# Moving two start loads ahead of the start barrier, with eight zero products for 14, in a decode attention kernel

## The chip, the cores and the metric

The kernel runs on one core of a Trainium2 chip. Its time is device microseconds (us) of that core, measured over a few executions. The profile's span is a little shorter than the time (652.0 us against 653.45 in the run that was profiled before the change), so spans are compared with spans and times with times.

## The reference

One decode step: a layer norm of x (4 rows of 448), attention with 16 query heads over 8 K/V heads and a cache of 8192 positions, and a small MLP mixer as a gate.

```python
xn = _layernorm(x)                       # x: (4, 1, 448)
q = (xn @ wq)                            # 16 heads of 256
scores = einsum("bhqd,bhkd->bhqk", q, k) * 256 ** -0.5     # k, v: (4, 8, 8192, 256) bf16
s = einsum("bhqk,bhkd->bhqd", softmax(scores), v) ... @ wo
g = _silu(mixer_mlp(xn, w1, w2, w3, w4)) # two norms, gelu; S = 1, so the shifted parts are zero
return x + s * g
```

K and V are 4 x 8 pairs of 4 MB. Everything that is read once adds up to 279 MB.

## The kernel before

SyncE issues nearly all loads on one queue: wq (3.7 MB), w3 and w4, the K of the first two heads, most of wo, then in turn a K and a V of 4 MB, each as soon as its buffer is free. There are two K and two V buffers. A "head" below is one of the 32 pairs of batch row and K/V head. ScalarE loads x (3.5 KB) itself.

The engines' programs start with a barrier that the compiler library puts in: every engine runs a drain (which raises a "gather" semaphore) and then waits for GpSimd's release (in the trace before, drains from 0.00 to 0.32 us, release at 0.61). A helper moves the first loads into that part:

```python
def begin_ahead(nc, loads):
    ...
    for load in reversed(loads):
        at = next(n for n, i in enumerate(first)
                  if i.engine == load.engine and isinstance(i, mybir.InstDrain))
        first.insert(at + 1, load)      # after the engine's arrival, before its wait
```

```python
def prog_sp(sp):
    ahead.append(sp.sem_inc(S["pause"], 1))       # two semaphore steps
    ahead.append(take(sp, "pause"))               # that only take time
    ahead.append(sp.dma_start(vflat[1][:, 0:DK * HDH], A_wq...).then_inc(S["dwq"], 16))
    ...                                           # w3, w4
    load_k(0); load_k(1); load_wo(NLATE, HQ, "dwo")
    for h in range(2, NH):
        load_k(h)                                 # waits v_k: head h-2 is transposed
        load_v(h - 2)                             # waits v_v: V buffer is free
    ...                                           # last V in four pieces, last wo in three
    sp.wait_ge(S["v_out"], 1)
    store(sp, 0)
    take(sp, "dout", 16 * NDG)

def prog_act(act):
    ahead.append(act.dma_start(x_sb[:, :], x2d).then_inc(S["dx"], 16))
```

On TensorE (PE) a prologue computes q and the MLP; then `NWARM` products of zeros follow, which only keep the array busy until the first K has landed. They are there for its clock: in the trace before they are 427 ns apart until 28.1 us and 217 after, and the clock records have full clock from 28.14:

```python
for i in range(NWARM):        # 14
    pe.matmul(psv[0:PVW, 0:QW], pT[:, 0, 0:PVW], wq_sb[:, 0, 0:QW], start=True, stop=True)
```

Each head then transposes K (L604 before, L612 after: the change shifts the lines by 8), multiplies, and multiplies with V. The last head's part (`finish`) has filler products of the same kind between its steps, `f_warm(n)`, 14 in all.

## Time and profile before

| what | value | read from |
|---|---|---|
| time, median of 3 | 653.85 us (653.24 to 654.89) | runs |
| span | 652.0 us | page |
| DMA | 279 MB, 428 GB/s mean | page |
| first packets of wq on the 16 engines | 1.26 to 2.12 us | list of DMA packets |
| third K load issued | 41.77 us | timeline |
| last piece of wo landed | 649.13 us | landings |

Here are the page's head and its rows for the whole DMA, which give in 40 equal slices the busy share in tenths and the rate:

```profile
span 652.0 us, 22813 instructions
PE 550.5 (84%) x9937; PEld 470.7 (72%) x9937; DVE 276.9 (42%) x622; ACT 255.8 (39%) x364; POOL 3.6 (1%) x17
DMA  9999999999999999999999999999999999999997
GB/s 374 440 420 433 430 434 434 430 438 426 440 426 440 426 440 426 440 428 436 432 435 430 434 434 426 440 426 440 426 440 428 438 428 438 430 436 430 434 429 301
```

DMA is full from the first slice to the last, while PE has a sixth of the span left. The waits of SyncE's queue (line, what it waited for, us in total, times, longest) say the same from the other side:

```profile
SPq L237 <- DVEq L515: 460.3, 30, 38.4
SPq L245 <- DVEq L483: 132.4, 31, 19.5
SPq L216 <- DVE out_b L544: 20.0, 1, 20.0
```

SyncE waits 460 us for K buffers, but that starves nobody: a load is issued 25 to 30 us before it lands, and landings are 9.7 us apart. The third line is the wait for the output.

The start, from the timeline (start, duration, engine, line, what, count, and in brackets the idle time before it and what ended it):

```profile
0.21 0.56 ACTq L312 DMA_DIRECT2D x_sb<-in_A_x_dram  x1
0.24 0.41 SPq L222 DMA_DIRECT2D vb<-in_A_wq_dram  x1
0.78 0.34 SPq L226 DMA_DIRECT2D vb<-in_B_w_dram  x1
2.01 0.38 DVE L385 CAST x_f<-x_sb 4x448 f32<-4x448 bf16 x1 [0.60 <-DMA x_sb<-in_A_x_dram]
...
23.94 5.26 PE L596 MATMUL psv<-vb,pT 128*32 128x512 bf16 x14
...
30.07 1.05 PE L604 MATMUL pst<-ident_b,kn 128*128 128x128 bf16 x16 [0.87 <-PEq L278]
...
41.77 0.33 SPq L237 DMA_DIRECT2D kn<-in_A_k_cache_dram  x1
```

The zero products fill 23.9 to 29.2, the first transposes start at 30.07 when K has landed, and the third K is issued at 41.77 when head 0 is transposed. And the end, the chain that ended last:

```profile
648.14 1.55 PE pst L703 x24
649.69 0.02 issue
649.72 0.40 DVE res L542
...
650.13 0.38 DVE out_b L544
```

PE's last products wait for the last piece of wo (649.13), so VectorE's closing instruction (`res`) starts 0.58 us after that landing.

### The profile page before, as it was taken

The page shows a single profiled execution, that of the slowest core. Times are in us where ns is not written, and L with a number is a line of the kernel's source. Part 1 is how long each engine was busy: PE and PEld are TensorE (multiplying, and loading weights), DVE is VectorE, ACT ScalarE, POOL GpSimd, SP SyncE. Part 2 cuts the span into 40 slices and gives each one's busy share as a digit, 9 for nine tenths or more (in the row PEclk, how much of TensorE's full clock was granted, in tenths as well). Part 3 has the DMA queues.
Part 4 walks back from the last instruction along what each step waited for, and adds up shares of the span by engine and source line. Part 5 has one row for each costly group of instructions (what it writes and reads, how often), then busy time and mean ns, then how long its engine had stood idle before and what let it go on. Part 6 is the DMA issues. An engine that isn't in the chain of part 4 may idle for free. (4 is left out here: it accounts for less than half of the span.)

```text
span 652.0 us, 22813 instructions
## 1 busy us (share of the span) xinstructions
PE 550.5 (84%) x9937; PEld 470.7 (72%) x9937; DVE 276.9 (42%) x622; ACT 255.8 (39%) x364; POOL 3.6 (1%) x17
## 2 busy tenths in 40 slices
PE   2799997988887987888897888898888798878897
PEld 1487876987676876667787766787677688757774
DVE  7344544343343443434443444444344344434442
ACT  4144543443343443323443333444234344423440
POOL 2000000000000000000000000000000000000000
PEclk9998999888799898889987888988779987978999
DMA  9999999999999999999999999999999999999997
GB/s 374 440 420 433 430 434 434 430 438 426 440 426 440 426 440 426 440 428 436 432 435 430 434 434 426 440 426 440 426 440 428 438 428 438 430 436 430 434 429 301
DMA packets 12353, 279.13 MB, mean 428 GB/s; under 512 B 1204, under 2 KB 3256, under 8 KB 3768
## 3 DMA queue, kind: packets, MB, share of 16 engines
q1 hardware_dynamic: 12328, 278.99, 99.5%
q8 instruction: 7, 0.11, 0.1%
q10 hardware_dynamic: 16, 0.01, 0.0%
q14 instruction: 2, 0.02, 0.0%
HBM read 278.99 MB, written 0.00 MB: 428 GB/s over the span
## 5 line engine op out<-in xcount | busy, mean ns | idle before, releaser
L604 PE MATMUL pst<-ident_b,kn 128*128 128x128 bf16 x4096 | 342.7, 237 | 81.4 <-PEq L278 79.3
L309 ACT ACTIVATE kT<-pst 128x1024 bf16<-128x1024 bf16 x224 | 229.3, 1024 | 357.5 <-ACTq L278 356.3
L604 PEld LDWEIGHTS pst<-ident_b,kn 128*128 128x128 bf16 x4096 | 271.7, 107 | 87.2 <-issue 86.6
L307 DVE COPY kT<-pst 128x1024 bf16<-128x1024 bf16 x288 | 197.5, 691 | 261.1 <-DVEq L278 261.1
L616 PE MATMUL psc<-qc,kT 128*128 128x2 bf16 x4096 | 178.2, 164 | 0.0
L616 PEld LDWEIGHTS psc<-qc,kT 128*128 128x128 bf16 x4096 | 157.1, 98 | 28.7 <-issue 28.5
L655 PE MATMUL psv<-vb,pT 128*4 128x512 bf16 x1056 | 85.6, 378 | 0.0
L634 PE MATMUL psm<-sel,po 128*128 128x2 f32 x272 | 36.8, 257 | 0.5 <-PEq L278 0.5
L634 PEld LDWEIGHTS psm<-sel,po 128*128 128x128 f32 x272 | 34.8, 196 | 0.9 <-issue 0.9
L655 PEld LDWEIGHTS psv<-vb,pT 128*4 128x4 bf16 x1056 | 21.8, 82 | 15.0 <-issue 0.4
L466 DVE TENSOR_REDUCE rmax<-psc 128x2 f32<-128x128 f32 x32 | 9.3, 292 | 48.1 <-DVEq L278 48.1
L484 DVE COPY po<-psv 128x512 f32<-128x512 f32 x34 | 23.5, 691 | 4.0 <-DVEq L278 3.3
L331 ACT ACTIVATE pT<-psc,negb 128x64 bf16<-128x64 f32 x66 | 20.6, 332 | 5.4 <-ACTq L278 5.4
L471 DVE TENSOR_REDUCE gmax<-psm 2x1 f32<-2x128 f32 x32 | 8.9, 279 | 32.3 <-DVEq L278 32.3
L628 PEld LDWEIGHTS psm<-diag,ones_f 2*128 2x128 f32 x66 | 13.5, 253 | 6.3 <-issue 5.0
L628 PE MATMUL psm<-diag,ones_f 2*128 2x2 f32 x66 | 16.2, 313 | 1.1 <-PEq L278 0.9
L331 ACT ACTIVATION_READ_ACCUMULATOR pT<-psc,negb 128x1 f32 x66 | 13.6, 206 | 0.0
L624 PEld LDWEIGHTS psm<-ident_f,rmax 128*2 128x2 f32 x32 | 2.6, 80 | 14.0 <-issue 14.0
L646 PE MATMUL psm<-rowsum,ones_f 128*128 128x2 f32 x64 | 11.6, 251 | 0.0
L552 PE MATMUL pst<-ident_b,xn_b 4*128 4x4 bf16 x14 | 0.6, 161 | 11.5 <-DVE xn_b L379 6.8
L646 PEld LDWEIGHTS psm<-rowsum,ones_f 128*128 128x128 f32 x64 | 9.5, 188 | 0.0
L474 DVE TENSOR_SCALAR diag<-ident_f,gmax 2x2 f32<-2x2 f32 x32 | 6.9, 217 | 4.8 <-DVEq L278 1.1
(101 smaller groups left out, 101.1 us busy)
## 6 DMA issues: line engine op xcount, KB each, us to landing
kn<-in_A_k_cache_dram SPq DMA_DIRECT2D x32, 4096.0 KB, 25.5
vb<-in_A_v_cache_dram SPq DMA_DIRECT2D x31, 4096.0 KB, 30.5
vb<-in_A_wq_dram SPq DMA_DIRECT2D x1, 3584.0 KB, 11.4
vb<-in_B_w_dram SPq DMA_DIRECT2D x2, 1568.0 KB, 16.3
wo_sb<-in_A_wo_dram SPq DMA_DIRECT2D x1, 2688.0 KB, 43.3
kn<-in_A_v_cache_dram SPq DMA_DIRECT2D x1, 2048.0 KB, 24.7
kn<-in_A_v_cache_dram SPq DMA_DIRECT2D x1, 1024.0 KB, 26.7
kn<-in_A_v_cache_dram SPq DMA_DIRECT2D x2, 512.0 KB, 27.9
```

Source lines behind the costliest of these rows:

```text
L307: engine.tensor_copy(dst, src).then_inc(S["v_ev"], 1)
L309: engine.activation(dst, src, ACT.Copy).then_inc(S["a_ev"], 1)
L331: ins = act.activation(pv_p[:, :, hh], sc[:, :, hh], ACT.Exp, bias=negb[:, s, hh:hh + 1], scale=SCALE, accum_out=rowsum[:, s, hh:hh + 1])
L466: v.tensor_reduce(rmax[:, :], psc[h % 2][:, 0:NCH * REP].rearrange("p (k h) -> p h k", h=REP), AX.X, ALU.max).then_inc(S["v_rmax"], 1)
L471: v.tensor_reduce(gmax[:, :], psm[0:REP, 0:P], AX.X, ALU.max).then_inc(S["v_s"], 1)
L484: v.tensor_copy(po[:, slot], psv[:, 0:CP * DH]).then_inc(S["v_po"], 1)
L604: ins = pe.transpose(dst[:, t * P:(t + 1) * P], kn[:, h % 2, GC * j + kl, half * P:(half + 1) * P], ident_b[:, :])
L616: ins = pe.matmul(psc[h % 2][:, kk * REP:(kk + 1) * REP], kT[:, j % RING, t * P:(t + 1) * P], qc[:, h % 2, half, :], start=(half == 0), st ...
L628: pe.matmul(psm[:, P:P + REP], ones_f[0:REP, :], diag[:, :], start=True, stop=True).then_inc(S["p_m2"], 1)
L634: ins = pe.matmul(dst(dh)[:, 0:width], po[:, slot, i * DH + dh:(i + 1) * DH:NHALF], sel[:, i, 0:width], start=(i == 0), stop=(i == CP - 1))
L646: pe.matmul(psm[:, P + REP:P + 2 * REP], ones_f[:, :], rowsum[:, h % 2, :], start=True, stop=True)
L655: ins = pe.matmul(psv[o:o + CP * REP, 0:CP * DH], pT[:, h % 2, kk * REP:(kk + CP) * REP], src[:, kk:kk + CP, :].rearrange("p c d -> p (c d)"),
```

## The change

Its intent is to start the stream of loads earlier. The wq load stands ahead of SyncE's drain and without the two pause steps; the x load heads ScalarE's program, ahead of its drain (in the diff it is the first of the two `loads`, and `later` puts ScalarE's former first two instructions behind it); there are eight zero products; the two pause steps stand in SyncE's closing part.

```diff
-    first = blocks[0].instructions
-    for load in reversed(loads):
-        at = next(n for n, i in enumerate(first)
-                  if i.engine == load.engine and isinstance(i, mybir.InstDrain))
-        first.insert(at + 1, load)
+    first = list(blocks[0].instructions)
+    for n, load in enumerate(loads):
+        own = [i for i in first if i.engine == load.engine]
+        drain = next(i for i in own if isinstance(i, mybir.InstDrain))
+        if n == 0:
+            later = own[0:2]
+            first = [i for i in first if i not in later]
+            at = first.index(drain)
+            first[at:at] = later
+            at = first.index(later[0])
+        else:
+            at = first.index(drain)
+        first.insert(at, load)
@@
-    NWARM = 14
+    NWARM = 8
@@ prog_sp
-            ahead.append(sp.sem_inc(S["pause"], 1))
-            ahead.append(take(sp, "pause"))
-            ahead.append(sp.dma_start(
+            ahead.insert(1, sp.dma_start(
@@
+            sp.sem_inc(S["pause"], 1)
+            take(sp, "pause")
             sp.wait_ge(S["v_out"], 1)
@@ prog_act
-            ahead.append(act.dma_start(x_sb[:, :], x2d).then_inc(S["dx"], 16))
+            ahead.insert(0, act.dma_start(x_sb[:, :], x2d).then_inc(S["dx"], 16))
```

## The prediction

> **What bounds it.** The DMA engines. The page's 40 slices show DMA at 9 tenths in all but the last, at 426 to 440 GB/s nearly throughout; 279.0 MB are read. In the list of DMA packets all 16 engines are active together for 638.8 of 652.0 us. PE is busy 84% but waits: SyncE's queue holds its K loads 460 us for buffers, yet each 4 MB load lands 25 to 30 us after issue and landings come 9.7 us apart, so the queue is two to three loads deep. The time is: the first wq packet's start (1.26 us into the span), about 646 us of packets, and the tail (last wo piece lands at 649.1, then DVE, the store and its receipt until 652.0).
>
> **What the change does.**
> 1. wq load. Before, SyncE runs its drain at 0.00 and two semaphore steps, and issues wq at 0.24 us (timeline of SyncE). After, the load is its first instruction: issue at about 0.00, first packet at about 1.0. The whole DMA stream moves 0.24 us earlier.
> 2. Barrier. SyncE now arrives after its 0.41 us of issue and ScalarE after 0.56 us of x issue (start about 0.13), so at about 0.7 in place of 0.32 (PE was last). Release moves from 0.61 to about 0.85, the w3 issue from 0.78 to about 1.0. wq's packets keep the engines busy until 10.7, so this is off the path. I take it that the drain does not wait for the data of a load in flight: no trace here shows a drain behind a load.
> 3. Eight zero products for 14. The timeline shows the 14 spaced 427 ns (half clock) until 28.1 us and 217 ns after. After: about 3.4 us of them, ending near 27.4 instead of 29.2; PE then waits for the first K, which landed at 29.94. [...] With eight it may not be granted in time. Estimate: head 0's 16 groups at 0.65 us would take up to 2.4 us longer. The third K load is issued when head 0's transposes are done, at 41.8; its packets start about 1.0 later, and the loads before it end at 44.35 (first engine) to 46.24 us (last). So 2.4 us of delay is absorbed where it counts: the last engine, which sets the time, doesn't idle.
> 4. The two semaphore steps move to where SyncE waits 20 us for the output: free.
>
> **On the path:** only the 0.24 us of step 1, and perhaps a few tenths either way from the engines' start order and instruction fetches (first packets start 1.26 to 2.12 us).
>
> **Predicted:** 653.6 us, 8 in 10 within 652.5 to 654.8 (the three runs before span 1.65 us). Faster by over 2%: 0.005; within 2%: 0.985; slower: 0.01.
>
> **What would show it.** Right: wq issue is SyncE's first record at about 0.0, first packets near 1.0; wq, first K and last wo landing 0.2 to 0.3 us earlier from the span's start; barrier release near 0.85; DMA at 9 throughout, same chain at the end. PE's idle before the first transposes grows from 0.9 to about 2.5 us; if those are 107 ns apart rather than 55, the third K issue moves towards 44 us without a dip in the second to fourth slice's GB/s. Wrong: w3 issued after wq landed (11 us): the drain waits for the load, and some us are lost.
>
> **What would make it wrong:** that drain; a cold PE late enough to empty the queue around 45 or 63 us; a shift in the run-to-run level; start-up before the span's first record absorbing the 0.24 us.

## The result, and the profile after

The changed kernel takes 653.92 us (median of 6, 653.32 to 654.52), the kernel before 653.73 in the six runs that stand beside it (653.24 to 654.89). The ratio is 1.0001, with a 95% interval of 0.9988 to 1.0014. Ratios here are ratios of mean times, not of the medians; those of the ten experiments come out of the lists of runs when the profiled run is left out. The interval is 0.8 us to either side, so the expected 0.24 us can't be seen in the times; only the traces can show it. The page after:

```profile
span 652.4 us, 22801 instructions
DMA  9999999999999999999999999999999999999997
GB/s 378 445 416 434 427 438 430 436 430 436 430 438 430 434 434 432 436 430 436 428 435 430 438 428 440 428 440 428 438 430 436 430 436 430 438 430 434 434 425 289
```

The start, in the timeline after:

```profile
0.00 0.41 SPq L228 DMA_DIRECT2D vb<-in_A_wq_dram  x1
0.12 0.57 ACTq L320 DMA_DIRECT2D x_sb<-in_A_x_dram  x1
1.11 0.33 SPq L232 DMA_DIRECT2D vb<-in_B_w_dram  x1
4.95 0.38 DVE L393 CAST x_f<-x_sb 4x448 f32<-4x448 bf16 x1 [3.17 <-DMA x_sb<-in_A_x_dram]
...
26.39 3.23 PE L604 MATMUL psv<-vb,pT 128*32 128x512 bf16 x8
...
29.87 1.05 PE L612 MATMUL pst<-ident_b,kn 128*128 128x128 bf16 x16 [0.25 <-PEq L286]
...
41.82 0.33 SPq L243 DMA_DIRECT2D kn<-in_A_k_cache_dram  x1
```

wq is issued 0.24 us earlier, its first packet starts at 1.04 in place of 1.26. But VectorE's first use of x moved from 2.01 to 4.95 us: **x arrives 2.9 us later**, although it is issued 0.09 us earlier. The whole prologue follows, and its products start at 26.4 in place of 23.9. Eight of them end at 29.6, just as the first K lands (29.74); head 0 starts 0.2 us earlier than before and the third K is issued at the same time. So the smaller count isn't a saving by itself: it pays for the late x.

The list of DMA packets in the trace shows why x is late. Times in us from the span's start:

```
                            before           after
first wq packets start      1.26 to 2.12     1.04 to 1.69, lasting 1.4 to 2.6
second wq packets start     2.85             2.73, lasting 1.1
x, four data packets        1.16 to 1.61     2.71 to 3.42
x, four completion writes   1.22 to 1.65     3.87 to 4.62
```

In the trace after, with wq's packets there first, each of x's four data packets starts within 0.01 us of the end of a wq packet of 1.6 to 2.3 us, and each of its four completion writes within 0.01 us of the end of one more, of 1.1 to 1.2 us. So I read it that x waited for two wq packets in turn.

Of the 0.2 us at the start, 0.16 are kept to the end in the mean of the 16 engines' landings (last wo: 648.06 before, 647.90 after). In this pair of runs the last engine kept 0.02 (649.13 and 649.11): it was 0.18 to 0.19 earlier up to an instruction fetch of 16 KB at 327.9 us, which takes one DMA engine 0.88 us and by the landings made another engine the last one. Nor is the 0.16 there in every run: in a second trace of the changed kernel (e10) the stream is 0.24 us earlier up to the third K, then loses as much at the fourth K (issued at 61.34 in place of 60.26), and the mean landing at the end is 648.07, against 648.06 before the change. Then the closing part came later. The chain after:

```profile
647.17 1.10 PE pst L763 x8
648.27 0.39 PE pst L721 x16
648.66 1.46 PE pst L711 x24
...
650.14 0.40 DVE res L550
...
650.56 0.38 DVE out_b L552
```

VectorE's `res` starts 1.03 us after the last landing in place of 0.58: PE itself was behind, not waiting. The reason stands in the granted clock (the share of its full clock that the profiler says PE was given; 0.50 is half clock) of the stretch in which the last head's K is transposed. The columns are the stretch, its length, busy time and instruction count of PE, PEld, DVE, ACT and POOL, then PE's granted clock, DMA share and GB/s. Before, then after:

```profile
617.70:624.00 6.30, 6.16 (x127) 6.07 (x127) 3.25 (x6) 4.57 (x8) 0.00 (x0) 1.00 0.99 427
```

```profile
617.70:624.00 6.30, 6.18 (x79) 6.00 (x80) 2.14 (x4) 2.79 (x7) 0.00 (x0) 0.58 1.02 442
```

The clock records show half clock for stretches of 3.4 or 6.8 us all through both runs. In the run before the last such stretch was at 598 to 605 us, in the run after at 616 to 623, inside the last head, whose transposes then took 13.5 us in place of 11.3. PE waits for that K in both runs, 1.8 us before the change and 4.5 after. What differs too is how the 3.4 us steps of the clock records (in both traces every stretch in them that ends within the span is a whole multiple of 3.41 us) lie over the wait (one step of the kernel before, then one of the changed kernel and the half clock that follows it):

```profile
615.20:618.60 3.40, 1.63 (x29) 0.96 (x18) 1.20 (x5) 0.00 (x0) 0.00 (x0) 1.00 1.05 453
```

```profile
612.80:616.20 3.40, 0.51 (x7) 0.08 (x1) 1.19 (x3) 0.00 (x0) 0.00 (x0) 1.00 1.03 443
616.20:623.00 6.80, 5.18 (x54) 5.00 (x54) 1.45 (x3) 1.89 (x2) 0.00 (x0) 0.50 1.02 439
```

PE was busy for 48% of the step before the change and kept its clock, for 15% after and lost it. The same count over the matmul records of all twelve traces, from 57 us on: in the step before a fall to half clock (273 falls) PE was busy for 57% at most, but for one of 71% (e8 at 644.5); in a step after which the clock stayed full, for 45% at least. The experiments come back to this: of the runs with the same start, some have the long stretch in the last head and some don't.

### The profile page after: what moved, and what is told of

Its sections match the earlier page's. It is cut to its first block, busy times and chain, and to the rows that moved or that the text cites. A ratio compares the mean times of both kernels' runs of the same rounds, so it can differ in the third digit from the quotient of the medians.

```text
span 652.4 us, 22801 instructions
## 1 busy us (share of the span) xinstructions
PE 550.7 (84%) x9931; PEld 472.6 (72%) x9931; DVE 276.8 (42%) x622; ACT 256.2 (39%) x364; POOL 3.6 (1%) x17
## 6 DMA issues: line engine op xcount, KB each, us to landing
vb<-in_A_wq_dram SPq DMA_DIRECT2D x1, 3584.0 KB, 11.5
```

## The experiments

Ten runs, in three calls. The kernel before ran beside them: 654.26 us in the first (median of 11), 653.64 in the second (9), 653.56 in the third (11). The calls ran on three chips; away from the places named below, the mean landings of all twelve traces keep their distances to a few hundredths of a us, so single traces can be compared.

**Theory A**: the DMA stream is the time. The change moved its start by 0.2 us and kept everything behind it as it was, because the fewer products match the late x. **Rival B**: PE sets the pace, since SyncE waits for it 460 us.

### e1: the loads alone

```diff
# against the changed kernel
-    NWARM = 8
+    NWARM = 14
```

> The changed kernel with 14 zero products put back, so only the order of the loads and the closing steps differ from the kernel before. Theory A (the DMA stream sets the time, PE has slack at the start): x still lands near 4.9 us, the prologue ends 2.5 us later than before, so the 14 products end near 31 us in place of 29.5, head 0's transposes start 1 to 2 us after the first K has landed (29.7), the third K is issued near 43 to 44 us in place of 41.8, and the time stays within 0.5 us of the kernel before. Rival B (PE sets the pace and releases the loads): the 1 to 2 us come out at the end, 654.7 to 655.7 us.

Measured: 654.50 us (653.23 to 655.18), ratio to before 1.0000 (0.9987 to 1.0013). The products and the first transposes, and the third K:

```profile
26.24 5.54 PE L604 MATMUL psv<-vb,pT 128*32 128x512 bf16 x14
31.71 1.07 PE L612 MATMUL pst<-ident_b,kn 128*128 128x128 bf16 x16
...
43.40 0.33 SPq L243 DMA_DIRECT2D kn<-in_A_k_cache_dram  x1
```

Head 0 starts 1.8 us late, as expected, and the third K is issued 1.6 us late. The delay was not absorbed in this trace: the mean landing of the third K is 0.86 us later than in the changed kernel, and every later mean landing to the end is later by the same 0.85 to 0.86. The span is 653.6. The times of the five runs don't resolve it, one of them being as fast as 653.23, so what the delay costs in every run is not settled by this run.

### e2: the products alone

```diff
# against the kernel before
-    NWARM = 14
+    NWARM = 8
```

> The kernel before with 8 zero products and nothing else. x lands near 2.0 us, the products end near 27.4 us and PE is idle for 2.5 us before the first K at 29.9. My prediction's step 3: the clock may be at half for head 0 (transposes 107 ns apart in place of 55), the third K issued up to 44 us; by theory A the time stays within 0.5 us of the kernel before all the same. If the clock is at full at 30 us, step 3's worry was empty even with the idle time.

Measured: 655.60 us (654.54 to 656.10), ratio 1.0020 (1.0007 to 1.0033): this half of the change, without the other, costs about 1.3 us.

```profile
24.08 3.15 PE L596 MATMUL psv<-vb,pT 128*32 128x512 bf16 x8
30.14 1.87 PE L604 MATMUL pst<-ident_b,kn 128*128 128x128 bf16 x16 [2.90 <-PEq L278]
...
43.13 0.33 SPq L237 DMA_DIRECT2D kn<-in_A_k_cache_dram  x1
```

With x early, eight products leave PE idle for 2.90 us. The 16 transposes then take 1.87 us in place of 1.05, that is 104 ns from one to the next in place of 56: half clock, from 30.0 to 33.4 us by the clock records. The clock had been full from 26.6 to 30.0: it came up while the eight products ran, and was at half after the 2.90 us of idle time. The third K goes out 1.4 us late, and the mean landing of the third K is 0.5 us later than before, kept to the end. This is the danger that the prediction's step 3 named; it comes true where x is early, and not in the changed kernel, where x is late.

### e3: x first again

```diff
# against the changed kernel
-            ahead.insert(1, sp.dma_start(
+            ahead.append(sp.sem_inc(S["pause"], 1))
+            ahead.append(take(sp, "pause"))
+            ahead.append(sp.dma_start(
```

> The changed kernel with the two semaphore steps again ahead of the wq load, both still ahead of SyncE's arrival at the barrier: wq is issued 0.16 us later, after x (0.12 us). Theory C (x landed late because wq's packets stood in all 16 engines before x's): x lands near 2.0 us in place of 4.9 and the prologue is 2.5 to 2.9 us earlier; first wq packets near 1.2. Rival D (x is late because of its place ahead of the barrier or in ScalarE's program): x stays near 4.9. Time within 0.5 us of the kernel before in either case.

Measured: 654.63 us (654.27 to 655.26), ratio 1.0007 (0.9994 to 1.0020). x landed at 1.53 us in place of 4.92:

```profile
0.13 0.56 ACTq L322 DMA_DIRECT2D x_sb<-in_A_x_dram  x1
0.17 0.40 SPq L230 DMA_DIRECT2D vb<-in_A_wq_dram  x1
...
1.70 0.37 DVE L395 CAST x_f<-x_sb 4x448 f32<-4x448 bf16 x1
...
30.27 1.05 PE L614 MATMUL pst<-ident_b,kn 128*128 128x128 bf16 x16 [2.50 <-PEq L288]
```

x stands where the change put it; only wq is 0.17 us later and so 0.04 behind x. That settles theory C against D: the order of the two issues decides, and 0.12 us of lead for wq cost x 2.9 us. With x early the eight products are too few again (2.50 us idle, half clock from 31.7), the third K goes out at 43.58. The stream ends 1.10 us later than before in the mean landing, 0.27 of it lost at the fourth K.

### e4: without the closing steps

```diff
# against the changed kernel
-            sp.sem_inc(S["pause"], 1)
-            take(sp, "pause")
             sp.wait_ge(S["v_out"], 1)
```

> The changed kernel without the two semaphore steps in SyncE's closing part. They run where SyncE waits 20 us for the output, so by theory A nothing moves: within 0.4 us of the changed kernel (653.9), the store issued 0.4 us after the last VectorE instruction as before. Rival: they hold SyncE's instruction count, and without them an instruction fetch falls into the closing part and adds some tenths of a us there.

Measured: 654.06 us (653.59 to 655.51), ratio to before 1.0003 (0.9991 to 1.0015). The profiled run has a span of 651.8, with the last landing at 648.98, `res` 0.58 us after it and the store issued 0.41 us after VectorE's last instruction started, as in both kernels. The steps cost nothing and save nothing that shows. This trace also shows the changed start where no late closing part hides it: 0.15 us earlier than before at the last landing, 0.2 in the span.

### e5: wq late on purpose

```diff
# against the kernel before
+            for _ in range(26):
                 ahead.append(sp.sem_inc(S["pause"], 1))
                 ahead.append(take(sp, "pause"))
```

> The kernel before with 26 pairs of semaphore steps ahead of the wq load in place of one: 50 more steps of 0.075 to 0.08 us, so wq is issued 3.8 to 4.0 us later and nothing else is slowed. If the stream's start counts one to one, the time is 3.8 to 4.0 us over the kernel before, about 658, and the last wo lands as much later from the span's start. Rival (start-up is absorbed somewhere, which would also have absorbed the change's 0.2 us): clearly under 3 us.

Measured: 656.70 us (656.59 to 656.79, four runs), ratio 1.0042 (1.0026 to 1.0057). A step took 0.063 us, less than I took, so wq was issued at 3.37 us:

```profile
3.37 0.40 SPq L223 DMA_DIRECT2D vb<-in_A_wq_dram  x1
```

That is 3.13 us later; the last wo landed 3.39 later (652.53), and the span is 3.4 longer. In the times it is 2.8 us over the mean of the kernel before and 3.4 over its fastest run (653.29). The interval of the ratio is 1.7 to 3.7 us, so the times alone don't rule out a part being absorbed; by the trace the start counts about one to one. The expectation of 3.8 to 4.0 was off by the length of a step.

### e6: more to load

```diff
# against the changed kernel
+    EXTRA, EXTRAS = 3072, (6, 12, 18, 24)
...
                 load_v(h - 2)
+                if h in EXTRAS:
+                    n = EXTRAS.index(h)
+                    if n:
+                        sp.wait_ge(S["dextra"], 16 * n)
+                    sp.dma_start(extra[:, :], A_k_cache[0, n]...[:, 0:EXTRA]
+                                 ).then_inc(S["dextra"], 16)
```

> The changed kernel with four more loads of 0.786 MB (3.15 MB in all, into a buffer that nobody reads), queued behind V loads in the middle of the run. Nothing waits for them but one another. Theory A (the DMA stream is the time): 3.15 MB at 433 GB/s are 7.3 us, so 661.2 us, within 0.7. Rival B (PE, 84% busy, sets the pace): PE has no more work, so under 1 us more.

Measured: 662.10 us (660.49 to 662.12), ratio to before 1.0125 (1.0109 to 1.0140), that is about 8 us more. In the profiled run, the fastest of the four, the last landing is 7.1 us later (656.22) and `res` follows it as before:

```profile
656.81 0.40 DVE res L557
```

All four runs lie just outside the expected 660.5 to 661.9, that one below and the other three, at 662.09 to 662.12, above; they kept no trace, and their 1.6 us more stay unexplained. PE has nothing more to do. Rival B falls: the stream is the time.

### e7: PE late on purpose

```diff
# against the changed kernel
-    NWARM = 8
+    NWARM = 32
```

> The changed kernel with 32 zero products in place of 8: 24 more at 217 ns (full clock from 29 us) put head 0's start at about 35 in place of 29.9, and the third K's issue at about 47 in place of 41.8. My prediction said that a delay is absorbed until the last engine runs dry (46.05 less 1.0 for the packets to start, that is a delay of 3.2 us): then 5.1 us cost 1.9, 655.8 us. Theory A2, from the two runs where head 0 was 1.4 to 1.6 us late and the last landing 0.5 to 0.7 us late (the first engine to run dry counts[...]): slack about 1.0 us, so 5.1 us cost about 4, 657.5 to 658.5 us. Rival B (PE sets the pace): all 5.1 us, 659.

Measured: 661.80 us (660.50 to 662.30), 1.0114 (1.0098 to 1.0129): about 7.5 us more, over every theory. The trace splits it. First, the third K is issued 6.2 us late, at 48.01 (head 0 started at 35.2, as expected, and took 0.9 us longer):

```profile
48.01 0.33 SPq L243 DMA_DIRECT2D kn<-in_A_k_cache_dram  x1
```

The mean landing of that K is 5.3 us later. Second, 2.5 us more are lost between the landings at 331 and 392 us. There PE stood still:

```profile
344.31 1.86 PE L612 MATMUL pst<-ident_b,kn 128*128 128x128 bf16 x16 [14.75 <-PEq L286]
```

The queue of 16 KB instruction fetches (PE's, as I infer from their times) has 17 fetches in this run in place of 7, nine of them between 333 and 385 us, where the program goes back to the head of the loop for its second half. What held PE for 14.75 us is not shown: the three fetches in that time took 0.96 to 2.1 us each, and what filled the rest stays open. No other run here has such a stop; in the changed kernel the longest wait there is 3.1 us. So my dose was not clean: it changed the program's size (22849 instructions on the page in place of 22801) and the number of fetches too.

The first part is clean, and with e1 to e3 it measures the slack that the prediction got wrong:

| run | third K issued, later than in the changed kernel | its mean landing, later |
|---|---|---|
| e2 (its stream starts 0.17 later) | 1.31 us | 0.67 us, 0.50 without that start |
| e1 | 1.58 us | 0.86 us |
| e3 (its stream starts 0.18 later) | 1.76 us | 0.96 us, 0.78 without that start (more at the fourth K) |
| e7 | 6.19 us | 5.27 us |

A delay costs its length less 0.7 to 1.0 us. The packets show both halves of that. In the changed kernel the first engine takes up the third K at 43.92; a load's packets start 0.96 us after its issue (e1: 43.40 and 44.36), so the slack is 43.92 - 0.96 - 41.82 = 1.1 us. And in e1 the engines that ran dry started anew with a slow packet: the third K's first packets lasted 1.4 to 2.2 us there on 14 engines, in place of 1.21 for most of them in the changed kernel.

### e8 and e9: the fillers at the end; e10: the changed kernel again

```diff
# e8, against the changed kernel: in f_warm, which finish() calls
-                for i in range(n):
+                for i in range(0):
```

> The changed kernel without the 14 filler products in the last head's part (4, 2, 2, 3 and 3 of about 0.2 us). In the changed kernel's profile PE was 2.2 us late there, after a stretch of half clock at 616 to 623 us, and VectorE's first closing instruction came 1.03 us after the last landing, in place of 0.58 in the kernel before. Theory E (the fillers are in the way when PE is late): the closing instruction comes 0.6 us after the last landing whatever the clock did before, mean time 0.2 to 0.5 us under the changed kernel's. Rival F (the fillers keep the clock up): half clock in the last 10 us, and the closing part 0.5 to 2 us longer.

Measured: 653.36 us, ratio to before 0.9990 (0.9977 to 1.0004); four runs at 653.21 to 653.42, and the profiled one at 655.14. In that one a half-clock stretch of 6.8 us fell into the last head and another on 644.5 us. Its chain has `res` 2.27 us after the last landing, and the clock of the last stretch is low:

```profile
649.00 2.40 PE pst L711 x24
...
651.43 0.40 DVE res L550
```

```profile
640.00:649.00 9.00, 7.94 (x106) 5.04 (x100) 2.17 (x4) 0.00 (x0) 0.00 (x0) 0.75 0.84 340
```

In the five traces where PE was late with its fillers in place (the changed kernel, e1, e2, e7, e10) the clock stays full in this part. So the fillers seem to keep it up when PE is late, by one trace without them against five with; the theory that they are only in the way falls.

```diff
# e9, against the changed kernel
-                f_warm(4)
...
-                f_warm(2)
...
-                f_warm(2)
```

> The changed kernel with six of the 14 filler products of the last head's part (the two groups of three that stand last) and without the first eight (4, 2 and 2). Without all 14, four runs of five were at 653.2 to 653.4 us and the profiled one at 655.1, with half clock from 644.5. Theory G (the first eight only delay a PE that is late, the last six keep the clock up): all runs at 653.1 to 653.6, none above 654.3, closing instruction 0.6 us after the last landing. Rival H (a run above 654.5 or a half-clock stretch in the last 10 us again): the fillers that were taken out were needed too.

Measured: 653.31 us, ratio 1.0004 (0.9988 to 1.0020): five runs at 653.13 to 653.33, one at 656.61, which kept no trace. That run goes against theory G, which allowed none above 654.3, and speaks for H, but its cause stays open.

> The changed kernel once more, on the same chip and in the same rounds as the run with six fillers, to put the two beside each other and to add to the comparison with the kernel before: 653.3 to 654.5, ratio to the kernel before 0.9990 to 1.0010. In the profile, the closing instruction comes 0.6 us after the last landing where no half-clock stretch falls on 612 to 640 us, and later where one does.

Measured: 653.26 us (653.12 to 654.71), ratio 0.9998 (0.9985 to 1.0011), as expected. The profiled run (654.71) has half clock in all of the stretch that was looked at above,

```profile
617.70:624.00 6.30, 5.77 (x63) 5.59 (x64) 1.81 (x4) 2.47 (x6) 0.00 (x0) 0.50 1.03 447
```

and `res` 1.46 us after the last landing. Over the twelve traces the rule holds without exception: where a 6.8 us half-clock stretch fell into the last head (the changed kernel, e1, e2, e7, e8, e10), `res` came 0.99 to 2.27 us after the last landing; where none did, or one of 3.4 us (the kernel before, e3, e4, e5, e6, e9), it came 0.58 or 0.59 us after it. Both traces of the changed kernel have the long stretch there, while e4 and e9, which start in the same way, have not, and the changed kernel's times (653.12 to 654.71) spread like those of the kernel before (653.21 to 655.00). So I take where the stretch falls, that is how the clock's 3.4 us steps lie over PE's wait for the last K, for chance of the run; that the program favours it is not excluded. No version here beats both kernels beyond the noise.

## Why the prediction was right, and where its steps were not

The time was right: 653.6 us with 652.5 to 654.8 forecast, 653.92 measured, and "within 2%" at 0.985. Its main reason held too: the stream of loads is the time (e6), its start counts about one to one (e5), and the rest of the change does not show in it. But that is in part luck. The prediction saw eight products behind an early x, which is about e3: its stream ended 1.10 us later than before. What kept the third K in its place was a late x that the prediction did not foresee. Besides, 0.24 us can't be told from nothing in these times. Point by point:

1. **wq earlier by 0.24 us**: right at the issue (0.00) and nearly at the first packet (1.04, 0.21 earlier). wq landed 0.12 earlier and the first K 0.20. "Last wo landing 0.2 to 0.3 us earlier" was too much: 0.16 in the mean over engines, 0.02 on the last one in this pair of runs, 0.15 in e4; in e10, the changed kernel again, 0.00 in the mean.
2. **The barrier**: the order was right, the size small: release at 0.98 us, forecast 0.85. Behind a load a drain takes 0.12 to 0.14 us in place of 0.01. It does not wait for the load's data, which land at 11.5. What failed is a step that the prediction left out: it gives x's issue ("start about 0.13", measured 0.12) and nothing on x's arrival, so that its step 3 has x there as early as before. x landed 2.9 us later, since wq's packets stood ahead of it (e3).
3. **The products**: "ending near 27.4" failed by that same late x; they ended at 29.6. That PE's idle "grows from 0.9 to about 2.5 us" failed: it fell to 0.25. That full clock might not be granted in time with eight was an estimate of mine: with 14 products the trace before has it from 28.1 us, after the 27.4 at which I saw the eight end. The cold clock did not occur in the changed kernel's trace (full from 29.1 us, the first transposes at 29.87). Where the idle time was there it came, by another way than forecast: the clock was granted in time and lost after 2.90 us of idle (e2). Granted late is what e6 shows, which has the changed kernel's start: half clock until 31.45, the first 16 transposes at 1.84 us in place of 1.05, and the third K issued 0.35 us later, which the stream absorbed. "2.4 us of delay is absorbed where it counts" was wrong, though the change did not put it to the test: the slack is about 1 us, not 3.2. I counted to the last engine's end; in e1 the early engines ran dry first and restarted slowly (first packets of 1.4 to 2.2 us), and what they lost stayed to the end (0.85 to 0.86 us in the mean landings).
4. **The closing steps are free**: right (e4).

The four parts of the change are not separate. Early wq makes x late (2.9 us); a late x makes the prologue late (its products start at 26.4 us in place of 23.9); eight products make up for it (ended at 29.6, the first K landed at 29.74). Either half alone issues the third K 1.4 to 1.6 us later (e1, e2), and together they leave it where it was.

## What to carry to other kernels

Where one queue of large loads bounds a kernel, look for what could leave that queue empty: here the third K had about 1 us of slack, and what e1 lost beyond it (0.85 to 0.86 us in the mean landings) stayed to the end. Issue a small load that others wait for before a large one: here, 0.03 to 0.04 us ahead it landed at 1.5 to 2.6 us in three traces (before, e2, e3), 0.12 us behind at 4.4 to 5.2 in eight. With so small a lead it is not quite undisturbed: with 3.2 us of lead (e5) it landed at 1.6. And tune fillers for the clock together with what comes before them, since what counts is the time left until the data land, not a number of products: the same eight left PE idle for 0.25 us behind the late x, and for 2.50 (e3) and 2.90 us (e2), followed by half clock, behind the early one.

## Figures that the traces gave

- From issue to first packet: wq's issue started at 0.00 and ended at 0.41 us, its first packet started at 1.04, that is 1.04 us from the start of the issue and 0.63 from its end. Before the change it was 0.24, 0.64 and 1.26: 1.02 and 0.62 us.
- The first packets of the third K on engines that had run dry took 1.4 to 2.2 us in e1, against 1.21 for most of the same packets in the unbroken stream of the changed kernel.
- In both kernels each of the seven 16 KB fetches (PE's, as inferred) took 0.88 to 0.96 us on a DMA engine, which a kernel bound by those engines can see: after the fetch at 327.9 the last landings of two loads lay 10.05 us apart in the kernel before and 10.21 in the changed one, in place of 9.7.
- A drain behind a load that was just issued took 0.12 us on SyncE and 0.14 on ScalarE, against 0.01 with nothing before it.
- 2.50 us (e3) and 2.90 us (e2) of idle PE were followed by half clock. In the traces before and after, the half-clock stretches between 30 us and the last landing were of 3.41 or 6.83 us.
